# Attention steps kept behind the drains of first products, in a fused attention and feed-forward kernel

## The chip, the cores and the metric

The kernel runs on one core of one Trainium2 chip. The metric is the device time of one execution in microseconds, lower is better. The median of three runs before the change is 853.23 us (850.61 to 854.34).

## The reference

Linear attention over 8 batches, 8 heads, 576 positions and 64 columns a head, then a gated feed-forward layer over all 4608 tokens:

```python
q_s = exp(q - max(q, -1));          q_s /= sum(q_s, -1) + 1e-9
k_s = exp(k - max(k, 2));           k_s /= sum(k_s, 2) + 1e-9      # over the 576 positions
kv  = einsum('bhsd,bhse->bhde', k_s, v)
x   = einsum('bhsd,bhde->bhse', q_s, kv)      # -> (4608, 512)
h   = x @ w_in                                # 512 x 2048
g   = h * erf(softplus(h))
out = g @ w_out                               # 2048 x 512
```

Inputs and output are 32-bit floats.

## The kernel before

**Steps.** The tokens are cut into 12 blocks of 384 (two batches make three blocks), the 2048 middle columns into 4 groups of 512. That makes 48 steps, numbered n = 0 to 47, block by block. Steps 0 to 3 run in 32-bit floats while the weights are read in; from step 4 on each operand is split into a high and a low 16-bit half and a product is the sum of three. The feed-forward layer works a step at a time:

- `mm1(n, k)`, k = 0 to 3, is the first product, done in seven smaller ones (a Strassen form), each of twelve matmuls of 128x192. They go through three banks of PSUM, called Y, X and Z, in the order Y, X, Z, X, X, Z, X. A bank must be read out ("drained") into the tile H before its next product may start. VectorE drains Y (L1011), the first X (L1013), the third X (L1021) and the second Z (L1024); ScalarE copies out the first Z (L1016) and the second and fourth X (L1018, L1026).
- `softplus` and `erf` run on ScalarE (all from L344, each with a load of its table), `gmul` (L1079), `ghi` (L1093) and `glo` (L1097) on VectorE; the last two leave the two 16-bit halves of G in the space of H. These are the letters T, G, U, I and O.
- `mm2(n, tt)` is the second product, for three tiles of 128 tokens, twelve matmuls of 128x512 each (L1125).

While step n's first product runs, step n-2's second product does, one tile of it behind each quarter of the first.

**Attention.** One generator, `attention_rest`, gives the work of batches 1 to 7 in pieces. A token "A" draws one piece: the maxima of k (L497 to L501), their transposes on TensorE (L508, L521) and the reduction (km, L512), the maximum and subtraction of q (L454, L455), the subtraction from k (L662, L667), the exponentials on ScalarE, the products of k and v (L542) and their scale (kvbd, L595, L596), the sums of q (L461 to L467), the two halves of q (L640, L641) that SP transposes by a DMA (L643), and the products with q that give x (L632), which ScalarE copies into the x block (L443). q of the tail positions of two batches is called qt and is worked on with the odd batch. `load_kv` and `load_q`, the loads of the next batch, are issued within the same pieces, on SP's queue. `finish` then splits an x block into halves and the sums of the Strassen form (L297 on ScalarE, L298 and L388 on VectorE).

**What sets the order.** The program is written in the order of a hand-made string of tokens up to step 3, and then by the loop at the end, which draws attention pieces by `pace` behind each tile of `mm2`. That order is only a priority: a scheduler at build time puts the instructions of each engine into a fixed queue, letting one that is ready by its own reckoning pass one that stands ahead of it but is not. So a piece of attention may run long before the place where it is drawn. Each engine then runs its queue in order.

From about 112 us the weights are split too: `wsplit` and `wsplit_sums` (tokens S and R) put 16-bit halves of w_in (wi) and w_out (wo) in place, ScalarE the high half (L297), VectorE the low half (L298) and the sums (L322).


Of the kernel before, what the change touches and what calls it, by code (L numbers as in the profile page):

```python
# [1 line left out]

# [11 lines left out]
ALU = mybir.AluOpType  # L14
# [43 lines left out]
def attn_moe_kernel(  # L58
# [9 lines left out]
    nc = tc.nc  # L68
# [123 lines left out]
    def wdecode(i, part=None):  # L192


        jn, a = divmod(i, NPC)
        if jn not in stg:
            if wjobs[jn] in raw_place:
                stg[jn] = raw_place[wjobs[jn]][:, :4096].bitcast(F32)
            else:
                stg[jn] = xp.tile([P, 2048], F32, tag="x7", name=f"sg_{jn}")  # L200
        d = stg[jn][:, a * 1024:(a + 1) * 1024].bitcast(I32)
        if part is None:
            r = raws[i].rearrange("p a n -> p (a n)").rearrange("p (n two) -> p n two", two=2)
        else:
            r = raws[i][:, :, 512 * part:512 * part + 512].rearrange(
                "p a (n two) -> p a n two", two=2
            )
            d = d.rearrange("p (a n) -> p a n", a=2)[:, :, 256 * part:256 * part + 256]
        lo, hi = r[..., 0], r[..., 1]
        nc.vector.tensor_scalar(  # L210
            d, hi, 5, 2, op0=ALU.logical_shift_left, op1=ALU.logical_shift_right,
        )
        nc.vector.scalar_tensor_tensor(
            d, lo, 29, d, op0=ALU.logical_shift_right, op1=ALU.bitwise_or
        )
        nc.vector.scalar_tensor_tensor(
            d, hi, -(2**30), d, op0=ALU.bitwise_and, op1=ALU.bitwise_or
        )
        if part == 0:
            return  # L220
        raws.pop(i)
        slots.append(held.pop(i))
        slots.sort(key=lambda x: x[1])
        wload()
# [5 lines left out]
    def wop(jn, h, i, n):  # L230

        o = h * WIN + i * 512
        return wplace[wjobs[jn]][:, o:o + n * 512].rearrange("p (n c f) -> p n c f", n=n, c=2)
# [5 lines left out]
    def wsquares(jn):  # L239

        which, g = wjobs[jn]
        o = NG * (which == "out") + g
        for i in range(4):
            nc.scalar.activation(
                sqs, stg[jn][:, i * 512:(i + 1) * 512], AF.Square, accum_out=sq4[:, o, i:i + 1]
            )
        wsq.add(jn)
# [52 lines left out]
    def wsplit(jn):  # L300


        which, g = wjobs[jn]
        s = w_s[which][:, g:g + 1]
        assert "all" in wready and not raws

        assert all(wplace[wjobs[jn]] is not raw_place.get(wjobs[j]) for j in stg)
        if which == "out":
            split2(stg.pop(jn), whalf(jn, 0), whalf(jn, 1), s)
            wdone(jn)  # L310
            return
        sg = stg[jn].rearrange("p (c f) -> p c f", c=4)
        A = {(i, j): sg[:, 2 * j:2 * j + 2, 256 * i:256 * i + 256]
             for i in range(2) for j in range(2)}
        hi, lo = (wop(jn, h, 0, 2).rearrange("p n c f -> p (n c) f") for h in range(2))
        split2(sg[:, :, :256], hi, lo, s)
        split2(A[1, 1], wop(jn, 0, 2, 1)[:, 0], wop(jn, 1, 2, 1)[:, 0], s)
        for o, x, y, op in (
            ((1, 1), (1, 0), (1, 1), ALU.add), ((1, 0), (0, 0), (1, 0), ALU.subtract),
            ((0, 0), (1, 1), (0, 0), ALU.subtract), ((0, 1), (0, 1), (0, 0), ALU.subtract),  # L320
        ):
            nc.vector.tensor_tensor(A[o], A[x], A[y], op=op)  # L322

    def wsplit_sums(jn):
        which, g = wjobs[jn]
        sg = stg.pop(jn).rearrange("p (c f) -> p c f", c=4)
        for i in range(2):
            hi, lo = (
                wop(jn, h, 3 + 2 * i, 2).rearrange("p n c f -> p (n c) f") for h in range(2)
            )  # L330
            split2(sg[:, :, 256 * i:256 * i + 256], hi, lo, w_s[which][:, g:g + 1])
        wdone(jn)
# [14 lines left out]
        return i  # L347

    emitted = set()


    bat = [dict() for _ in range(B)]
# [461 lines left out]
    def attention_rest():  # L814
        for b in range(1, B):
            yield from attention(b) if b < E32 else attention16(b)

    att = attention_rest()

    def warm(n):  # L820

        z = ident.bitcast(F16)
        wm = pso.tile([P, 512], F32, tag="o2", name=f"warm_{n}")
        for _ in range(2 * n):
            nc.tensor.matmul(wm[:, :256], z[:, :P], z, start=True, stop=True)
# [149 lines left out]
    def mm1(n, k):  # L975

        p, bk, g = seq[n]
        s = st[n]  # L980
        assert ("in", g) in wready
        x = x7[p * NBK + bk]
        jn = wjobs.index(("in", g))
        Th = T // 2
        if k == 0:
            s["H"] = ch.tile([P, FG, T], F32, tag="H", bufs=3, name=f"H_{n}")
        C = {(i, j): s["H"][:, 2 * i:2 * i + 2, Th * j:Th * j + Th]
             for i in range(2) for j in range(2)}

        def prod(b, wi, xi):  # L990
            new = b not in s
            if new:
                s[b] = psh.tile([P, 512], F32, tag=f"p{b}", name=f"p{b}_{n}")
            w = [wop(jn, h, wi, 1)[:, 0] for h in range(2)]
            for a in range(2):
                o = s[b][:, a * Th:(a + 1) * Th]
                for c in range(2):
                    for i, (wl, xl) in enumerate(((0, 0), (0, 1), (1, 0))):
                        nc.tensor.matmul(  # L999
                            o, w[wl][:, c, a * P:(a + 1) * P], x[:, xl, xi, c, :],  # L1000
                            start=(new and a == 0 and c == 0 and i == 0),
                            stop=(c == 1 and i == 2), skip_group_check=True,
                        )

        def bank2(b):
            return s[b][:, :T].rearrange("p (a t) -> p a t", a=2)

        add = nc.vector.tensor_tensor
        if k == 0:
            prod("Y", 1, 1)  # L1010
            nc.vector.tensor_copy(C[0, 0], bank2("Y"))  # L1011
            prod("X", 0, 0)
            add(C[0, 0], bank2("X"), C[0, 0], op=ALU.add)  # L1013
        elif k == 1:
            prod("Z", 6, 3)
            nc.scalar.copy(C[1, 1], bank2("Z"))  # L1016
            prod("X", 3, 6)
            nc.scalar.copy(C[0, 1], bank2("X"))  # L1018
        elif k == 2:
            prod("X", 5, 5)  # L1020
            add(C[1, 1], bank2("X"), C[1, 1], op=ALU.add)  # L1021
        else:
            prod("Z", 4, 2)
            add(C[0, 1], bank2("Z"), C[0, 1], op=ALU.add)  # L1024
            prod("X", 2, 4)
            nc.scalar.copy(C[1, 0], bank2("X"))  # L1026

# [124 lines left out]
    def tok(name):  # L1152

        if name != "A":
            if name in done:
                return
            done.add(name)
        if name in steps:
            dep, f = steps[name]
            assert all(x in emitted_steps for x in dep.split()), name  # L1160
            f()
            emitted_steps.add(name)
            if all(f"y{c}" in emitted_steps for c in range(NC4)):
                bat[0]["xdone"] = True
            return
        c = name[0]
        if c == "A":
            r = next(att, None)
            share[0] += r or 0
            return r  # L1170
        x = [int(i) for i in name[1:].split(".")] if name[1:] else []
        if c == "w":
            warm(*x)
        elif c == "D":
            wdecode(NPC * x[0] + x[1], *x[2:])
        elif c == "Q":
            wsquares(*x)
        elif c == "S":
            wsplit(*x)
        elif c == "R":  # L1180
            wsplit_sums(*x)
        elif c == "f":
            xready(x_next[0])
            finish(x[0] % 2)
        elif c == "Z":
            wscales()
        elif c == "m":
            (mm1_32 if x[0] < NG else mm1)(*x)
            emitted.add(("m", *x))
        elif c == "M":  # L1190
            mm2(*x)
            emitted.add(("M", *x))
        else:
            fn[c](*x)

    def xready(i):

        p, bk = divmod(i, NBK)
        for b in [(2 * p,), (2 * p, 2 * p + 1), (2 * p + 1,)][bk]:
            while "xdone" not in bat[b]:  # L1200
                assert tok("A"), i
# [18 lines left out]
    for o in ORDER.split():  # L1220
        tok(o)
# [54 lines left out]
```

## Time and profile before

| | |
|---|---|
| median of three runs | 853.23 us |
| the profiled execution | 853.86 us |
| its span, first to last instruction | 851.7 us |
| mean granted TensorE clock | 0.988 |
| TensorE busy | 811.2 us (95%) |
| VectorE busy | 638.2 us (75%) |
| ScalarE busy | 503.0 us (59%) |
| GpSimd busy | 17.6 us (2%) |
| moved by DMA | 62.59 MB |

The busy times are shares of the whole span; a line of the profile such as "DVE H L1021 <- PE pX L999" says that VectorE's instruction of line 1021, writing H, waited for TensorE's of line 999, writing pX. PE is TensorE, PEld its weight loads, DVE VectorE, ACT ScalarE, POOL GpSimd, SPq the DMA queue of SyncE.

### The profile page before, as it was taken

To read this page: it belongs to the slowest core of one execution; us is meant where nothing else is said; L and a number is where in the kernel's file an instruction comes from. 1 tells how busy PE (TensorE), PEld (TensorE's weight loads), DVE (VectorE), ACT (ScalarE), POOL (GpSimd) and SP (SyncE) were. 2 spreads that over 40 slices of the span, in tenths; PEclk is the share of its full clock that TensorE was granted. 3 is DMA by queue.
4 is the path that set the end of the run, shared out by engine and by line. 5 is a ranking of instruction groups with operands and counts; after the bars stand their busy time and mean duration, and the time that the engine had idled before them with its cause. 6 is when DMAs were issued, how large, how long until landed. Compare 5 with 4: busy or idle time off the path is not lost.

```text
span 851.7 us, 15370 instructions
## 1 busy us (share of the span) xinstructions
PE 811.2 (95%) x6448; PEld 553.8 (65%) x6448; DVE 638.2 (75%) x913; ACT 503.0 (59%) x633; POOL 17.6 (2%) x37
## 2 busy tenths in 40 slices
PE   2999998899999999999999999999999999999997
PEld 1655557567667667766776676766776676777673
DVE  5999899998997879758865779748866657554543
ACT  2598486777564556555673566555663565543532
POOL 2010000000000000000000000000000000000000
PEclk8899999899999999999999999999999999999999
DMA  9997420016416402412134302322121000100100
GB/s 255 407 250 197 120 75 13 1 25 112 106 35 131 108 9 61 103 31 51 51 70 98 87 14 51 93 51 51 38 51 38 38 2 1 38 1 1 38 1 37
DMA packets 145508, 62.59 MB, mean 73 GB/s; under 512 B 134688, under 2 KB 136736, under 8 KB 145440
## 3 DMA queue, kind: packets, MB, share of 16 engines
q1 hardware_dynamic: 143264, 53.23, 25.1%
q0 software_dynamic: 2176, 8.39, 2.8%
q8 instruction: 50, 0.82, 0.4%
q14 instruction: 18, 0.15, 0.1%
HBM read 45.09 MB, written 9.44 MB: 64 GB/s over the span
## 4 chain that ended last, share of the span: by engine, by line
PE 64%; DVE 19%; ACT 10%; issue 3%; SPq 2%; DMA 1%; ACTq 0%; POOL 0%; DVEq 0%
PE o L1125 27%; PE pX L999 15%; PE pZ L999 7%; ACT G L344 4%; PE o L1116 4%; ACT L344 3%; PE pY L999 3%; DVE G L1079 3%; PE kv L542 2%; DVE H L1097 2%; PE pX L1038 2%; DVE H L1093 2%; SPq L409 2%; PE x L632 1%; DVE wi L298 1%
## 5 line engine op out<-in xcount | busy, mean ns | idle before, releaser
L1125 PE MATMUL o<-wo,H 128*128 128x512 f16 x1584 | 367.0, 380 | 2.8 <-DVE H L1093 1.8
L999 PEld LDWEIGHTS <-wi 128*128 128x128 f16 x3696 | 311.2, 98 | 44.3 <-issue 15.7
L1125 PEld LDWEIGHTS <-H 128*128 128x128 f16 x1584 | 152.7, 98 | 157.4 <-DVE H L1093 2.6
L999 PE MATMUL pX<-x,wi 128*128 128x192 f16 x2112 | 206.2, 248 | 7.6 <-ACT H L1018 4.5
L344 ACT ACT_TABLE_LOAD x104 | 133.4, 1283 | 2.8 <-DVE H L1024 0.8
L1079 DVE SCALAR_TENSOR_TENSOR G<-G,small,H 128x1536 f32<-128x1536 f32 x44 | 79.9, 1817 | 56.2 <-ACT G L344 56.0
L1026 ACT COPY H<-pX 128x384 f32<-128x384 f32 x44 | 20.9, 475 | 165.3 <-PE pX L999 159.9
L999 PE MATMUL pZ<-x,wi 128*128 128x192 f16 x1056 | 104.0, 247 | 3.4 <-ACT x L297 1.8
L344 ACT ACTIVATE G<-H,U 128x768 f32<-128x768 f32 (+1 forms) x60 | 72.7, 1231 | 22.1 <-DVE H L1024 21.5
L1097 DVE TENSOR_TENSOR H<-G,H 128x1536 f16<-128x1536 f32 x44 | 77.2, 1755 | 1.0
L344 ACT ACTIVATE G<-G 128x1536 f32<-128x1536 f32 x48 | 71.2, 1484 | 0.5
L999 PE MATMUL pY<-x,wi 128*128 128x192 f16 x528 | 51.9, 247 | 0.0
L1024 DVE TENSOR_TENSOR H<-pZ,H 128x384 f32<-128x384 f32 x44 | 24.4, 554 | 32.5 <-PE pZ L999 32.1
L1011 DVE COPY H<-pY 128x384 f32<-128x384 f32 x44 | 24.3, 553 | 30.3 <-PE pY L999 30.3
L1116 PE MATMUL o<-wo,G 128*128 128x512 f32 x96 | 43.4, 597 | 0.0
L1093 DVE CAST H<-G 128x1536 f16<-128x1536 f32 x44 | 42.1, 957 | 0.8
L297 ACT ACTIVATE x<-x 128x768 f16<-128x768 f32 (+1 forms) x44 | 32.9, 763 | 12.8 <-DVE x L388 11.1
L1141 DVE TENSOR_SCALAR ob<-o,V 128x512 f32<-128x512 f32 x29 | 21.7, 748 | 24.5 <-PE o L1125 24.5
L298 DVE SCALAR_TENSOR_TENSOR x<-x,x 128x768 f16<-128x768 f32 (+1 forms) x44 | 37.0, 851 | 3.2 <-ACT x L297 3.2
L1013 DVE TENSOR_TENSOR H<-pX,H 128x384 f32<-128x384 f32 x44 | 24.4, 554 | 15.9 <-PE pX L999 15.7
L443 ACT ACTIVATE x<-x 128x384 f32<-128x384 f32 (+1 forms) x52 | 17.5, 394 | 30.0 <-PE x L632 27.4
L1116 PEld LDWEIGHTS o<-wo,G 128*128 128x128 f32 x96 | 17.5, 190 | 18.7 <-issue 18.2
(184 smaller groups left out, 762.7 us busy)
## 6 DMA issues: line engine op xcount, KB each, us to landing
out_dram<-ob SPq DMA_DIRECT2D x32, 256.0 KB, 2.4
vbuf<-in_v_dram SPq DMA_DIRECT2D x60, 128.0 KB, 3.1
q<-in_q_dram SPq DMA_DIRECT2D x56, 128.0 KB, 3.4
k<-in_k_dram SPq DMA_DIRECT2D x56, 128.0 KB, 3.1
wo<-in_moe_w_in_dram SPq DMA_DIRECT2D x4, 1024.0 KB, 17.2
wi<-in_moe_w_out_dram POOLq DMA_DIRECT2D x2, 1024.0 KB, 8.9
wi<-in_moe_w_in_dram SPq DMA_DIRECT2D x2, 1024.0 KB, 9.4
raw<-in_moe_w_out_dram POOLq DMA_DIRECT2D x2, 1024.0 KB, 8.0
```

The source lines that it names most:

```text
L297: nc.scalar.activation(hi, src, AF.Copy, scale=s)
L298: nc.vector.scalar_tensor_tensor(lo, src, s, hi, op0=ALU.mult, op1=ALU.subtract)
L344: i = nc.scalar.activation(out_, in_, func, **kw)
L999: nc.tensor.matmul(o, w[wl][:, c, a * P:(a + 1) * P], x[:, xl, xi, c, :], start=(new and a == 0 and c == 0 and i == 0), stop=(c == 1 and i ...
L1011: nc.vector.tensor_copy(C[0, 0], bank2("Y"))
L1013: add(C[0, 0], bank2("X"), C[0, 0], op=ALU.add)
L1024: add(C[0, 1], bank2("Z"), C[0, 1], op=ALU.add)
L1079: nc.vector.scalar_tensor_tensor(flat(s["G"]), flat(s["G"]), (GB if n in OUT32 else GA)[:, g:g + 1], flat(s["H"]), op0=ALU.mult, op1=ALU.mult,
L1093: nc.vector.tensor_copy(flat(s["gh"]), flat(s["G"]))
L1097: nc.vector.tensor_tensor(flat(s["gl"]), flat(s["G"]), flat(s["gh"]), op=ALU.subtract)
L1116: nc.tensor.matmul(o, s["G"][:, a, ts_], w[:, a, :], start=(first_ and a == 0), stop=(last_ and a == FG - 1),)
L1125: nc.tensor.matmul(o, s[gt][:, a, ts_], w[wl][:, a, :], start=(first_ and a == 0 and i == 0), stop=(last_ and a == FG - 1 and i == 2),)
```

## The change

Three drains that VectorE does are remembered as they are written: Y of k = 0, the third X of k = 2, and the second Z of k = 3. Whenever a piece of attention is drawn, every VectorE instruction in it gets an edge to the last one remembered, without a semaphore: the scheduler may not put it in VectorE's queue ahead of that drain. Pieces drawn before step 4's first product, those of batch 1, have nothing remembered and stay as they were; so do the token lists for splits and `finish`, and the attention's instructions on other engines.

```diff
+    drained = [None]
...
         if k == 0:
             prod("Y", 1, 1)
-            nc.vector.tensor_copy(C[0, 0], bank2("Y"))
+            drained[0] = nc.vector.tensor_copy(C[0, 0], bank2("Y")).ins
...
         elif k == 2:
             prod("X", 5, 5)
-            add(C[1, 1], bank2("X"), C[1, 1], op=ALU.add)
+            drained[0] = add(C[1, 1], bank2("X"), C[1, 1], op=ALU.add).ins
         else:
             prod("Z", 4, 2)
-            add(C[0, 1], bank2("Z"), C[0, 1], op=ALU.add)
+            drained[0] = add(C[0, 1], bank2("Z"), C[0, 1], op=ALU.add).ins
...
         if c == "A":
-            r = next(att, None)
+            with tc.issue_after(drained[0]) if drained[0] is not None else nullcontext():
+                r = next(att, None)
```

No instruction is added on any engine but for rows that the listing groups otherwise. What moves is the order, and with it that of the other engines, since the scheduler reckons all of them together. Lines from 350 on are one higher in the changed kernel, from 1169 on two. In the names below H_895, H_1011, H_1129, H_1304 are the tiles H of steps 4, 5, 6 and 7, H_2432 and H_2697 those of steps 13 and 14, G_n the tile G that goes with the H behind the arrow.

The first place is ScalarE's queue at the start of step 4. x_1 is x block 1, wo_95 the place of a group of output weights. Before:

```order
L297 ACTIVATE x_1_837<-x_138 128x768
L297 ACTIVATE wi_90<-wi_91,small 128x512
L297 ACTIVATE x_1_837<-x_138 128x768
L1016 COPY H_895<-pZ_924 128x2x192
L297 ACTIVATE wi_90<-wi_91,small 128x1024
L1018 COPY H_895<-pX_910 128x2x192
L297 ACTIVATE wi_90<-wi_91,small 128x1024
L297 ACTIVATE wi_91<-wi_92,small 128x1024
L297 ACTIVATE wi_91<-wi_92,small 128x512
L1016 COPY H_1011<-pZ_1041 128x2x192
L1026 COPY H_895<-pX_910 128x2x192
```

And in the changed kernel, on the same engine from the same place:

```order
L297 ACTIVATE wi_90<-wi_91,small 128x512
L297 ACTIVATE wo_95<-wo_96,small 128x2048
L297 ACTIVATE x_1_837<-x_138 128x768 x2
L297 ACTIVATE wi_90<-wi_91,small 128x1024
L1017 COPY H_895<-pZ_924 128x2x192
L297 ACTIVATE wi_90<-wi_91,small 128x1024
L1019 COPY H_895<-pX_910 128x2x192
L297 ACTIVATE wi_91<-wi_92,small 128x1024
L297 ACTIVATE wi_91<-wi_92,small 128x512
L1027 COPY H_895<-pX_910 128x2x192
```

The split of an output weight has moved from some thirty rows later to a place ahead of both splits of x block 1, and the copy of step 5's first Z (H_1011) has left; it now stands eight rows further down, behind step 4's softplus and erf.

The second place is VectorE's queue between the halves of step 5 and those of step 6. x_2 and x_791 belong to x block 2, km, q_0 and k_0 to batch 2. Before:

```order
L1024 TENSOR_TENSOR H_1129<-pZ_1184,H_1129 128x2x192
L298 SCALAR_TENSOR_TENSOR x_2_1159<-x_791,x_2_1159 128x768
L298 SCALAR_TENSOR_TENSOR x_2_1159<-x_791,x_2_1159 128x384
L1097 TENSOR_TENSOR H_1011<-G_1122,H_1011 128x1536
L388 TENSOR_TENSOR x_791<-x_791 128x2x192
L1011 COPY H_1304<-pY_1305 128x2x192
L388 TENSOR_TENSOR x_791<-x_791 128x2x192
L1013 TENSOR_TENSOR H_1304<-pX_1319,H_1304 128x2x192
L388 TENSOR_TENSOR x_791<-x_791 128x2x192
L662 TENSOR_TENSOR k_0_592<-k_0_592,kB_1346 128x1024
L388 TENSOR_TENSOR x_791<-x_791 128x2x192
L1079 SCALAR_TENSOR_TENSOR G_1297<-G_1297,small,H_1129 128x1536
```

And in the changed kernel:

```order
L1098 TENSOR_TENSOR H_1011<-G_1122,H_1011 128x1536
L389 TENSOR_TENSOR x_791<-x_791 128x2x192
L513 TENSOR_REDUCE km_1264<-kT_1259 128x4
L389 TENSOR_TENSOR x_791<-x_791 128x2x192
L455 TENSOR_REDUCE q_0_m<-q_0_800 128x16
L389 TENSOR_TENSOR x_791<-x_791 128x2x192
L456 TENSOR_TENSOR q_0_800<-q_0_800,q_0_m 128x1024
L389 TENSOR_TENSOR x_791<-x_791 128x2x192
L298 SCALAR_TENSOR_TENSOR x_2_1159<-x_791,x_2_1159 128x768
L1025 TENSOR_TENSOR H_1129<-pZ_1184,H_1129 128x2x192
```

Step 6's last sum, which stood three rows ahead of step 5's low half, now stands nine rows behind it, and the reduction of km and the maximum and subtraction of q, done much earlier before, stand between.

The third place is VectorE's queue in step 14. x_4 is x block 4, q_0 and q_1 the halves of batch 4's q. Before:

```order
L454 TENSOR_REDUCE q_0_m<-q_0_2638 128x16
L298 SCALAR_TENSOR_TENSOR x_4_2727<-x_1809,x_4_2727 128x768
L455 TENSOR_TENSOR q_0_2638<-q_0_2638,q_0_m 128x1024
L1079 SCALAR_TENSOR_TENSOR G_2693<-G_2693,small,H_2432 128x1536
L298 SCALAR_TENSOR_TENSOR x_4_2727<-x_1809,x_4_2727 128x768
L1093 CAST H_2432<-G_2693 128x1536
L454 TENSOR_REDUCE q_1_m<-q_1_2655 128x16
L1097 TENSOR_TENSOR H_2432<-G_2693,H_2432 128x1536
L1021 TENSOR_TENSOR H_2697<-pX_2712,H_2697 128x2x192
```

And in the changed kernel:

```order
L298 SCALAR_TENSOR_TENSOR x_4_2727<-x_1809,x_4_2727 128x768
L1080 SCALAR_TENSOR_TENSOR G_2693<-G_2693,small,H_2432 128x1536
L298 SCALAR_TENSOR_TENSOR x_4_2727<-x_1809,x_4_2727 128x768
L1094 CAST H_2432<-G_2693 128x1536
L1098 TENSOR_TENSOR H_2432<-G_2693,H_2432 128x1536
L1022 TENSOR_TENSOR H_2697<-pX_2712,H_2697 128x2x192
```

The three pieces of attention ahead of the third X drain have gone behind it, to the next step. From step 16 on TensorE's own queue is the same in both but for a few rows; on VectorE attention goes on to stand a few rows later.

More of the change, by code (lines that the diff above doesn't have):

```diff
@@ L1 @@
-from contextlib import ExitStack
+from contextlib import ExitStack, nullcontext
 import concourse.bass as bass
```

## The prediction

> **What bounds the kernel now.** I read the cores first, then busy time by stretch, then what TensorE waits for, then the order of time around its longest waits.
>
> ```profile
> core 0: 851.7 us, clock 0.988
> ...
> core 0: us, PE busy (x) PEld busy (x) DVE busy (x) ACT busy (x) POOL busy (x), PEclk, DMA share, GB/s
> ...
> 120.00:162.00 42.00, 33.56 (x234) 24.45 (x234) 40.41 (x52) 31.60 (x40) 0.96 (x1) 0.88 0.11 32
> 162.00:822.00 660.00, 651.12 (x5621) 459.16 (x5620) 481.38 (x677) 386.53 (x453) 3.16 (x10) 1.00 0.22 51
> ```
>
> The second of the rows, from 162 us, holds most of the span: TensorE is busy 651.1 of 660 us at full clock, VectorE 481. The first, 120 to 162 us, is the other way round: VectorE 40.4 of 42, TensorE 33.6, its clock 0.88. There the weights are split and the first half-precision steps start, and VectorE is the bound. The last two attention-free steps show the floor of a step:
>
> ```profile
> 733.49 2.59 PE o L1125 x12
> ...
> 748.18 2.59 PE o L1125 x12
> ...
> PE pX L999 <- ACT H L1018: 4.5, 2, 4.2
> ...
> DVE k L497 <- DMA k<-in_k_dram: 5.2, 3, 2.3
> ...
> PE pX L999 <- DVE H L1021: 1.5, 3, 0.9
> PE pX L999 <- ACT H L1026: 1.3, 2, 0.6
> ```
>
> The same group of twelve second products comes 14.69 us apart: nothing to be had there but by less work. The waits are small. The drains of first products, which the change puts in front of attention, cost TensorE 4.5 + 1.5 + 1.3 = 7.3 us in the whole run, 4.2 of them in one wait. So a change of order can gain a few us at most, unless it also shortens 120 to 162 us; and it can lose there, where VectorE has no idle time.
>
> **The change, part by part.** No instruction's work is added or taken away; no DMA is added. Every price is a place in VectorE's queue, so I follow three places, by the orders quoted above.
>
> *Head, the weight split in front.* VectorE's first batch 2 work is gone from before step 4:
>
> ```profile
> 126.42 0.69 DVE L497 TENSOR_TENSOR k<-k 128x512 f32<-128x512 f32 x1
> 127.02 1.21 DVE L454 TENSOR_REDUCE q_m<-q 128x16 f32<-128x1024 f32 x1
> ...
> 125.42 2.02 ACT L297 ACTIVATE wo<-wo,small 128x2048 f16<-128x2048 f32 x1
> ...
> 134.09 1.07 PE L999 MATMUL pZ<-x,wi 128*128 128x192 f16 x11 [1.28 <-DVE x L298]
> ...
> 135.20 0.48 ACT L1016 COPY H<-pZ 128x384 f32<-128x384 f32 x1 [2.68 <-PE pZ L999]
> ...
> 191.81 2.25 DVE L298 SCALAR_TENSOR_TENSOR wo<-wo,small,wo 128x2048 f16<-128x2048 f32 x1
> ...
> 152.79 2.08 PE L999 MATMUL pX<-x,wi 128*128 128x192 f16 x12 [4.19 <-ACT H L1018]
> ```
>
> What takes the room is splits of output weights: on ScalarE one of 2.02 us now stands ahead of the last two splits of x block 1, whose second half TensorE waits for at 134.09. Late by 2.0, caught up in the 2.68 us that ScalarE idles behind it. VectorE's half of that split (2.25, now run at 191.81) comes in ahead of step 4's third X drain, where one k maximum of 0.69 leaves: 2.25 - 0.69 = 1.6 at most, 1.3 if a few of the tenths that VectorE waits there are filled. Step 4's last product starts that much later. Then ScalarE's copy of step 5's first Z bank stands behind the erf of step 4, and TensorE, which now asks for that bank ahead of the products of 152.79, waits as it does now for the copy behind it: its 4.2 us wait stays, shifted by about 1 us. I book +1.3 by 178 us, and nothing for the pieces of attention that left: they come back below.
>
> *Head, x block 2 and step 6.*
>
> ```profile
> 171.79 0.55 DVE L1024 TENSOR_TENSOR H<-pZ,H 128x384 f32<-128x384 f32 x1
> ...
> 173.59 1.75 DVE L1097 TENSOR_TENSOR H<-G,H 128x1536 f16<-128x1536 f32 x1
> 175.26 0.55 DVE L388 TENSOR_TENSOR x<-x 128x384 f32<-128x384 f32 x1
> 175.73 0.55 DVE L1011 COPY H<-pY 128x384 f32<-128x384 f32 x1
> ...
> 161.45 0.68 DVE L512 TENSOR_REDUCE km<-kT 128x4 f32<-128x512 f32 x1
> ...
> 173.97 1.76 ACT L344 ACTIVATE G<-H,U 128x768 f32<-128x768 f32 x2
> 175.75 1.28 ACT L344 ACT_TABLE_LOAD   x1
> 177.05 1.49 ACT L344 ACTIVATE G<-G 128x1536 f32<-128x1536 f32 x1
> ...
> 179.19 1.81 DVE L1079 SCALAR_TENSOR_TENSOR G<-G,small,H 128x1536 f32<-128x1536 f32 x1
> ...
> 182.66 0.95 DVE L1093 CAST H<-G 128x1536 f16<-128x1536 f32 x1
> ...
> 186.39 1.74 DVE L1097 TENSOR_TENSOR H<-G,H 128x1536 f16<-128x1536 f32 x1
> ...
> 189.57 1.67 PE L1125 MATMUL o<-wo,H 128*128 128x512 f16 x7
> ...
> 194.32 0.69 PE L542 MATMUL kv<-vbuf,k 128*64 128x65 f32 x16
> ...
> 195.63 1.17 PE L999 MATMUL pZ<-x,wi 128*128 128x192 f16 x12
> ```
>
> Today the last sum of step 6 (L1024, 171.79) runs before step 5's low half (L1097, ends 175.3). In the new order it comes after that, after four differences of x (0.47 each, the distance of 175.26 and 175.73), the reduction for km (0.68), batch 2's q maximum and its subtraction (1.21 each by the row at 127.02) and a split of x (0.87). That is 1.88 + 0.68 + 2.42 + 0.87 = 5.9 us, less some 0.3 of overlap at the starts: it ends at 175.3 + 5.6 + 0.5 = 181.4, with L1097 where it is now. ScalarE's second half of the softplus waits for it: 0.9, then table 1.28 and erf 1.49 bring 185.1. VectorE then has L1079 1.81, kt 0.68, L1093 0.95, three attention pieces of 1.2 and L1097 1.74: 193.9, with 0.6 of small ones 194.5, where it now ends at 188.1. TensorE now reads that low half with its third product, at 190.0 (189.57 + 2 x 0.216, the twelfth part of 2.59). It would be held 4.5 us; but the new order moves the second kv product (194.32 to 195.63, 1.3 us) in front, so 3.2 remain. This wait swallows the +1.3 before it, since it hangs on VectorE and not on where TensorE was. Lower end 0, if VectorE reaches 181 some 3 us earlier by idle time I don't see; upper end 9.6 us (181.4 less 171.8) less the 1.9 slack and 1.3: +6.4. I take **+3.2**.
>
> *Later, the drains.*
>
> ```profile
> 255.17 1.07 PE L999 MATMUL pX<-x,wi 128*128 128x192 f16 x11 [0.34 <-ACT H L1018]
> ...
> 305.40 1.21 DVE L454 TENSOR_REDUCE q_m<-q 128x16 f32<-128x1024 f32 x1
> 306.52 1.75 DVE L1097 TENSOR_TENSOR H<-G,H 128x1536 f16<-128x1536 f32 x1
> 308.19 0.55 DVE L1021 TENSOR_TENSOR H<-pX,H 128x384 f32<-128x384 f32 x1
> ...
> 308.80 1.15 PE L999 MATMUL pX<-x,wi 128*128 128x192 f16 x12 [0.86 <-DVE H L1021]
> ...
> 343.53 1.15 PE L999 MATMUL pX<-x,wi 128*128 128x192 f16 x12 [0.64 <-ACT H L1026]
> ...
> 288.09 0.23 PE L632 MATMUL xt<-qt,kvbd 128*128 128x64 f16 x2 [0.94 <-DVE kvbd L595]
> ```
>
> At step 14 the q maximum (1.21) leaves the queue ahead of L1021, and that sum is then over before the bank is asked for: the wait of 0.86 goes, -0.9. Step 11's copy on ScalarE (0.34) comes 0.5 earlier, as a cast stands behind it now: -0.3. At 343.53, and one period later, ScalarE's copy waits behind a split of x, which waits for VectorE; a cast of k and q now stands ahead of that difference, so I book -0.2 each of the 0.64, not the whole. At 288.09 a maximum of k (0.69) enters the chain from the scale to kvbd, and five first products of about 0.08 come in ahead of the wait: +0.3, or 0.4 with the other wait of that place. Nothing is booked for the loads that SP issues behind the pinned steps. They go out later, as do the maxima that read them, and VectorE waits for such loads of k today, 5.2 us in three places, with TensorE busy: a maximum that comes later waits less. A load as late as the step itself shifts nothing. What is late next is the transposes of qt, a rival below. Sum -1.2, bounds -3.0 (the three drains' waits and the one at 288.09 gone, the second period's too) and +1.5 (0.69 in each of two more chains).
>
> **The sum**: +3.2 - 1.2 = +2.0. The profiled execution took 853.86 us, 2.2 beyond its span; it would take 855.9. The median of the runs shown is 853.23, 0.6 below it, so 855.2 beside that.
>
> [...] The row of 152.79 shows 2.08 us for twelve products that take 1.15 elsewhere, right behind 4.19 us of idle; the mean clock of that stretch is 0.88. [...]
>
> **Rivals.**
>
> ```profile
> 156.15 2.12 PE L999 MATMUL pX<-x,wi 128*128 128x192 f16 x12
> ```
>
> - *Faster: the head runs smoother.* If the order breaks the 4.19 us wait up and step 6 is in time, TensorE gains 3.4 of it and 1.9 of the two slow groups (2.08 and 2.12 for 1.15 each), with the drains' -1.2: 853.2 - 6.5 = 846.7. For it: batch 2's maxima (0.69 and 1.21 among them) have left VectorE ahead of step 5. Against: as much weight splitting has come in its place. It decides at 152.8: the wait must fall under about 1 us.
> - *No loss in the head.* VectorE reaches step 6 early enough for the 1.9 us of slack and the moved kv product: 853.2 - 1.2 = 852.0.
> - *Slower by more: the upper end.* Step 6's delay shows in full and steps 7 and 8 inherit some: +6.4 - 1.2, 858.4, with another 1.5 from one drain per late step 860. It decides at L1024 of step 6: if it ends after 184 us.
> - *Late transposes in the odd batches.* The last piece of qt is now pinned behind a drain, and its transpose on SP's queue behind that, so that TensorE could stand still for it in batches 3, 5 and 7.
>
> ```profile
> qt<-kt SPq DMA_TRANSPOSE x3, 3.1
> ```
>
> It takes 3.1 us to land; where it is issued only as TensorE gets there, it costs that less the 0.94 waited at 288.09 anyway, 2.2, and three times 6.5: 861. At half, 858. Against: in batches 5 and 7 the order leaves two groups of second products (2.59 each) and four of first ones between.
>
> **How the numbers follow.** Forecast, 853 to 857.4: 0.46. No loss: 0.25. Faster: 0.07. Slower cases together: 0.22. About 0.5%, 4.3 us, is what can be told from no change here; so faster is below 849.0, slower above 857.5. Same takes the first two, 0.71. The range leaves out the lower part of the faster case and the upper part of the slower ones, some 0.15: 849.5 to 859.5. The likeliest case gives 855.2.
>
> **What would show it.** In the changed kernel's trace: L1024 of step 6 (the third of its line) near 181 instead of 171.8; the third L1097 ending near 194; TensorE idle in front of the third group of second products; step 14's wait for L1021 gone; two waits for L1026 of about 0.4; TensorE's busy time after 200 us unchanged but for that. I am wrong if the third L1097 ends before 190, if the wait near 153 is under 3 us, or if TensorE waits for a transpose after 400 us.

## The result, and the profile after

The changed kernel takes 859.96 us (median of 6 runs, 858.73 to 861.49), the kernel before 853.57 us beside it: a ratio of 1.0085, 95% interval 1.0069 to 1.0101. It is slower, by 7.3 us by the ratio (the two medians lie 6.4 us apart); 855.2 was forecast, and the range ended at 859.5. The profiled execution took 861.49 us, with a span of 859.4.

The core, then the same two stretches as before (us; busy time of TensorE, its weight loads, VectorE, ScalarE, GpSimd; TensorE's clock; DMA share; GB/s):

```profile
core 0: 859.4 us, clock 0.992
...
120.00:162.00 42.00, 31.70 (x214) 23.74 (x213) 40.46 (x49) 30.47 (x38) 0.96 (x1) 0.84 0.11 32
162.00:822.00 660.00, 646.99 (x5574) 455.41 (x5572) 483.74 (x679) 381.15 (x449) 3.17 (x10) 1.00 0.22 51
```

VectorE is as full as it was up to 162 us (40.46 of 42, before 40.41), TensorE does 1.9 us less there, and then 4.1 us less than before in the next 660. What it waits for (line waited for: us in all, times, longest):

```profile
PE pZ L1000 <- ACT H L1017: 4.7, 1, 4.7
...
PE pZ L1000 <- ACT x L297: 3.7, 1, 3.7
PE pX L1000 <- ACT H L1019: 3.6, 4, 1.5
PE xt L633 <- DMA qt<-kt: 1.6, 2, 1.1
...
PE pX L1000 <- ACT H L1027: 1.1, 2, 0.5
PE pX L1000 <- DVE H L1022: 1.0, 2, 0.7
```

The wait of 4.2 at 152.8 has become one of 4.7 for the first Z's copy, and one of 1.78 us for a split of x block 1 (at 132.57 before) one of 3.7. Before, that row was:

```profile
132.57 0.24 PE L999 MATMUL pZ<-x,wi 128*128 128x192 f16 x1 [1.78 <-ACT x L297]
```

New are waits of up to 1.5 us for L1019, the copy of the fourth product, at 423 and 618 us, which stood nowhere in the forecast. To see where the time went, I take the start of each step's first product (the first pY row of the step), subtract that of the kernel before, and see by how much the difference grows over a stretch of steps; a gain is negative:

| stretch | after, minus before, us | forecast |
|---|---|---|
| steps 4 to 10 | +4.27 | +3.2 (the head) |
| steps 10 to 18 | -0.53 | -0.9 (step 14), -0.3 (step 11), -0.2, +0.4 (batch 3) |
| steps 18 to 23 | +1.72 | 0 |
| steps 23 to 32 | -0.03 | -0.2 |
| steps 32 to 35 | +1.73 | 0 |
| steps 35 to 47 | -0.01 | 0 |

(The rest of 7.41 us at step 47, 0.27, lies before step 4.) So the head came out 1.1 us above its forecast, and two losses of 1.7 us each, at steps 20 to 21 and 32 to 33, are what was not seen. The rows of the first of them, in the changed kernel (start, duration, engine, line):

```profile
409.49 0.55 DVE L1022 TENSOR_TENSOR H<-pX,H 128x384 f32<-128x384 f32 x1
...
409.96 1.21 DVE L455 TENSOR_REDUCE q_m<-q 128x16 f32<-128x1024 f32 x1
...
411.09 0.68 DVE L513 TENSOR_REDUCE km<-kT 128x4 f32<-128x512 f32 x1
...
411.69 1.21 DVE L456 TENSOR_TENSOR q<-q,q_m 128x1024 f32<-128x1024 f32 x1
...
412.82 0.55 DVE L1025 TENSOR_TENSOR H<-pZ,H 128x384 f32<-128x384 f32 x1
...
413.44 1.28 ACT L344 ACT_TABLE_LOAD   x1 [1.68 <-DVE H L1025]
...
420.79 2.00 ACT L344 ACTIVATE k<-k 128x1024 f32<-128x1024 f32 x2
422.70 0.46 ACT L1019 COPY H<-pX 128x384 f32<-128x384 f32 x1
...
423.20 1.15 PE L1000 MATMUL pX<-x,wi 128*128 128x192 f16 x12 [1.52 <-ACT H L1019]
...
618.47 1.15 PE L1000 MATMUL pX<-x,wi 128*128 128x192 f16 x12 [1.52 <-ACT H L1019]
```

Batch 5's first q is pinned behind step 20's third X sum (L1022), so its maximum and subtraction stand between that and the step's last sum (L1025). ScalarE waits 1.68 us for that sum, its softplus and erf are late, step 21's copies stand behind the erf (that of the fourth product also behind a second exponential of k, some 0.9 us, which follows it in the kernel before), and TensorE waits 1.52 us for the bank of the fourth product. Twelve steps later the same (618.47). The same place in the kernel before:

```profile
406.41 0.69 DVE L512 TENSOR_REDUCE km<-kT 128x4 f32<-128x512 f32 x1
...
407.01 0.55 DVE L1024 TENSOR_TENSOR H<-pZ,H 128x384 f32<-128x384 f32 x1
...
407.64 1.28 ACT L344 ACT_TABLE_LOAD   x1
...
415.95 0.46 ACT L1018 COPY H<-pX 128x384 f32<-128x384 f32 x1
...
416.46 1.15 PE L999 MATMUL pX<-x,wi 128*128 128x192 f16 x12
```

Only km's reduction stands there, ScalarE starts without a wait, and TensorE gets its bank in time. The forecast's own two places, in the changed kernel: the head (wo is VectorE's low half of an output weight's split, the row at 195.58 the third group of second products going on with the low half of G) and step 14.

```profile
127.75 2.35 DVE L298 SCALAR_TENSOR_TENSOR wo<-wo,small,wo 128x2048 f16<-128x2048 f32 x1 [0.75 <-ACT wo L297]
...
134.76 0.24 PE L1000 MATMUL pZ<-x,wi 128*128 128x192 f16 x1 [3.70 <-ACT x L297]
...
178.08 1.21 DVE L455 TENSOR_REDUCE q_m<-q 128x16 f32<-128x1024 f32 x1
...
179.67 1.22 DVE L456 TENSOR_TENSOR q<-q,q_m 128x1024 f32<-128x1024 f32 x1
...
182.14 0.55 DVE L1025 TENSOR_TENSOR H<-pZ,H 128x384 f32<-128x384 f32 x1
...
193.69 1.75 DVE L1098 TENSOR_TENSOR H<-G,H 128x1536 f16<-128x1536 f32 x1
...
195.58 2.55 PE L1126 MATMUL o<-wo,H 128*128 128x512 f16 x11
...
311.77 0.55 DVE L1022 TENSOR_TENSOR H<-pX,H 128x384 f32<-128x384 f32 x1
...
312.82 1.15 PE L1000 MATMUL pX<-x,wi 128*128 128x192 f16 x12
```

Step 6's last sum is at 182.14 (forecast 181.4, before 171.79), its low half over at 195.4 (forecast 194.5), and at 312.82 the wait of 0.86 for the third X sum is gone.

### The profile page after: what moved, and what is told of

It reads as the page before. It is cut to its first block, busy times and chain, and to the rows that moved or that the text cites. A ratio compares the mean times of both kernels' runs of the same rounds, so it can differ in the third digit from the quotient of the medians.

```text
span 859.4 us, 15376 instructions
## 1 busy us (share of the span) xinstructions
PE 813.1 (95%) x6448; PEld 555.5 (65%) x6448; DVE 640.9 (75%) x913; ACT 503.1 (59%) x633; POOL 17.6 (2%) x37
## 4 chain that ended last, share of the span: by engine, by line
PE 60%; DVE 18%; ACT 15%; issue 3%; SPq 2%; DMA 1%; ACTq 0%; POOL 0%; DVEq 0%
PE o L1126 25%; PE pX L1000 14%; PE pZ L1000 7%; ACT G L344 6%; ACT L344 5%; PE o L1117 3%; DVE G L1080 3%; PE pY L1000 3%; PE kv L543 2%; DVE H L1098 2%; PE pX L1039 2%; PE x L633 2%; DVE H L1094 1%; DVE x L298 1%; SPq L410 1%
## 5 line engine op out<-in xcount | busy, mean ns | idle before, releaser
L1025 DVE TENSOR_TENSOR H<-pZ,H 128x384 f32<-128x384 f32 x44 | 24.3, 553 | 33.7 <-PE pZ L1000 33.6
```

The lines of the kernel that those rows point to most:

```text
L1025: drained[0] = add(C[0, 1], bank2("Z"), C[0, 1], op=ALU.add).ins
```

## The experiments

All are edits of the changed kernel on the line numbers of the kernel before (L1018 is the fourth product's copy, L1024 the last sum, L1021 the third X sum). `at_n` is the step whose first product was written last. The ratios are to the kernel before, with their 95% intervals; the changed kernel's is 1.0085. The last column is worked out as in the table above, each from its one profiled execution.

| | ratio | interval | steps 4-10, 10-18, 18-23, 32-35, us |
|---|---|---|---|
| changed | 1.0085 | 1.0069 to 1.0101 | +4.27, -0.53, +1.72, +1.73 |
| e1 batch 2 free | 1.0033 | 1.0016 to 1.0050 | +0.01, -0.49, +1.72, +1.72 |
| e2 batch 2 alone | 1.0058 | 1.0035 to 1.0081 | +4.26, +1.64, +0.11, +0.02 |
| e3 q free in 5, 7 | 1.0041 | 1.0026 to 1.0057 | +4.11, -0.53, +0.03, +0.05 |
| e4 copy first | 1.0079 | 1.0057 to 1.0100 | +4.23, -0.52, +1.64, +1.65 |
| e5 q free in 2 | 1.0054 | 1.0034 to 1.0074 | +1.80, -0.49, +1.72, +1.72 |
| e6 pin Y only | 1.0011 | 0.9999 to 1.0023 | +2.89, -1.06, -0.17, -0.16 |
| e7 step 15 only | 0.9984 | 0.9970 to 0.9999 | -0.51, -1.51, +0.09, +0.04 |
| e8 late, q free | 1.0003 | 0.9990 to 1.0017 | +0.02, -0.50, +0.03, +0.04 |
| e9 wo split late | 1.0126 | 1.0110 to 1.0142 | +5.81, -0.55, +1.73, +1.73 |
| e10 Y from 15 | 0.9987 | 0.9973 to 1.0001 | +1.00, -1.38, -0.17, -0.16 |
| e11 wo_94 behind x1 | 1.0075 | 1.0052 to 1.0099 | +4.40, -0.52, +1.72, +1.71 |

e7 and e10 run the order of the kernel before in steps 4 to 10 (e1 and e8 up to 203 us), so the column's first number differs by -0.5 to +1.0 us between executions of one order. TensorE's granted clock goes with it: over the first 48 us of step 4 it is 0.93 in e7, 0.89 in the kernel before, e1 and e8, and 0.86 in e10. The other numbers repeat within a few hundredths.

**Theory:** the loss is two things. In the head, batch 2's attention, pinned behind step 6's drains, makes step 6's last sum late. In steps 20 and 32 the first q of batches 5 and 7 does the same. **Rivals:** the late waits are the head's loss seen again; or any pin crowds VectorE, wherever it is.

*e1 and e2, the two halves.*

```diff
-            with tc.issue_after(drained[0]) if drained[0] is not None else nullcontext():
+            pin = drained[0] is not None and at_n[0] >= 9     # e2: at_n[0] < 9
+            with tc.issue_after(drained[0]) if pin else nullcontext():
```

> Nothing is pinned while step 8 or an earlier one is under way, so batch 2 goes as in the kernel before; batches 3 to 7 are pinned. Theory (two separate losses: 4.2 us in the head by step 6's late last sum, 3.4 us by two waits of TensorE for ScalarE's copy of the fourth product, X of steps 21 and 33): the head's loss goes, the two waits stay at about 1.5 each, and the time is 1.7 to 2.7 us over the kernel before. Rival (the head's loss is only handed on, and later waits are the same idle time seen again): the later waits shrink with it, and the time is within 1 us of the kernel before.

> The other half: pinned only while step 8 or an earlier one is under way, so batch 2 alone is pinned. Theory: step 6's last sum stays at about 182 us and its low half ends at about 195; the time is 3.5 to 4.7 us over the kernel before, with no wait for the fourth product's copy at 420 or 615 us. Rival (the loss of the head is made up by idle time later on): under 2 us over.

e1 is 2.8 us over (0.33% of 852), e2 4.9 us over, together 7.7, about what the change costs (7.3). In e1 the head's +4.27 is gone and the two later losses stand unchanged at 1.72; in e2 the head stays and they are gone. They are two separate things: the first rival falls. (e2 has +1.64 in steps 10 to 18, as it doesn't get step 14's gain and waits 1.31 us there for L1021.)

*e3, the piece with the first q of batches 5 and 7 not pinned.*

```diff
+        free[0] = b in (5, 7)
         yield next(sh)
         km = k_max_T(b, kmax)
         q_sub(rows(qs[0]), 16, f"q_{b}_0")
+        free[0] = False
...
+            pin = drained[0] is not None and not free[0]
```

> As changed, but the one piece of batches 5 and 7 that holds km and the first q's maximum and subtraction is not pinned. By the order VectorE then runs those two (2.4 us) a step earlier, ahead of the last sum of step 19 and 31, and nothing of q stands between the third X sum and the last sum of steps 20 and 32. Theory (these two rows alone make the last sum 1.7 us late, softplus and erf with it, and TensorE waits for the copy queued behind the erf): both waits of 1.5 us go, and the time is 3.0 us over the kernel before, 3.4 under the changed kernel. Rival (VectorE is too full everywhere once attention stands late; another drain is late instead): at most 1 us under the changed kernel.

3.5 us over the kernel before, 0.44% (3.7 us) under the changed one. The timeline of e3 at step 20:

```profile
407.80 0.55 DVE L1024 TENSOR_TENSOR H<-pZ,H 128x384 f32<-128x384 f32 x1
...
409.02 1.28 ACT L344 ACT_TABLE_LOAD   x1
...
417.33 0.46 ACT L1018 COPY H<-pX 128x384 f32<-128x384 f32 x1
...
417.90 1.15 PE L999 MATMUL pX<-x,wi 128*128 128x192 f16 x12
```

No wait of ScalarE, none of TensorE. The order differs from the changed kernel's by these rows and what follows from them at the two places alone, so two rows of VectorE (1.21 each) in the wrong one of two slots are the whole 3.4 us. What follows from them is also that ScalarE's copy comes ahead of the second exponential and four of TensorE's second products behind the bank's first products; e4 has these two moves without VectorE's, and keeps the loss. The second rival falls.

*e4, ScalarE's copy ahead of the second exponential.* The exponentials of batches 5 and 7 behind k's first half are collected and issued in `mm1(n, 1)` right behind the copy of L1018.

```diff
             nc.scalar.copy(C[0, 1], bank2("X"))
+            [f() for f in late]; late.clear()
...
-            act(t, t, AF.Exp, chain=b > 1)
+            f = lambda t=t: act(t, t, AF.Exp, chain=b > 1)
+            late.append(f) if b in (5, 7) and t is not ks[0] else f()
```

> As changed, but in batches 5 and 7 the exponentials of the second half of k and of what follows it are issued behind ScalarE's copy of the fourth product of steps 21 and 33 instead of ahead of it; VectorE's and TensorE's queues stay. Theory: of the 1.7 us that TensorE loses at each place, the exponential ahead of the copy makes 0.94 and the late last sum the rest, so that the wait falls from 1.5 to about 0.6 and the time by 1.9 us under the changed kernel. Rival 1 (the late sum alone): the wait stays at 1.5, no change. Rival 2 (the order on ScalarE alone): the wait goes, 3.4 us under the changed kernel.

No gain to speak of: 0.08 us at each place. Against the changed kernel this tells little. e4's profiled execution runs 2.47 us ahead of the changed kernel's at step 18, so its copy (419.28 against 422.70) is 0.95 earlier; and yet TensorE waits 1.45 us:

```profile
415.60 2.75 PE L1125 MATMUL o<-wo,H 128*128 128x512 f16 x12
...
419.28 0.46 ACT L1018 COPY H<-pX 128x384 f32<-128x384 f32 x1
...
419.80 1.15 PE L999 MATMUL pX<-x,wi 128*128 128x192 f16 x12 [1.45 <-ACT H L1018]
```

TensorE's queue did not stay, as I had written: four second products (0.86 us), which the changed kernel has ahead of this wait, came behind it. TensorE started to wait as much earlier as the copy came. Against e3 it tells more: by their traces, from 80 us on, ScalarE's and TensorE's queues stand in the same order in e3 and e4, and VectorE's differs at the two places alone. There e3 loses 0.03 and 0.05 us, e4 1.64 and 1.65. So VectorE's rows by themselves make 1.6 of the 1.7 at each place. What the order on ScalarE would do with TensorE's queue held still stays open.

*e5, the q pieces of batch 2 not pinned* (as e3, with b = 2, and `q_sub` of the second q too).

> As changed, but the two pieces of batch 2 with the maxima and subtractions of q (and km) are not pinned. The early part of the head stays as in the changed kernel by the order (the split of an output weight ahead of x block 1's on ScalarE, TensorE held 3.7 us there); of the rows between the third X sum and the last sum of step 6 the first q's maximum and subtraction go, two of four differences of x and one split of x too: 2.4 + 0.9 + 0.9 = 4.2 us. Theory (the head's loss hangs on step 6's last sum, and the early delay is swallowed): the last sum at about 178 us instead of 182, the low half over at about 191.5 instead of 195.4, and the time 3 us under the changed kernel, some 4 over the kernel before. Rival (the early delay of 2.9 us carries through by itself): the last sum comes earlier, and the time is at most 1.5 us under the changed kernel.

2.6 us under the changed kernel by the ratios, 2.5 by the head's column (+1.80). Its last sum and low half of step 6:

```profile
174.90 0.55 DVE L1024 TENSOR_TENSOR H<-pZ,H 128x384 f32<-128x384 f32 x1
...
187.21 1.75 DVE L1097 TENSOR_TENSOR H<-G,H 128x1536 f16<-128x1536 f32 x1
```

With 1.9 us added, by which this execution starts step 4 ahead of the changed kernel's, 176.8 and 190.9: the last sum 5.3 us earlier, more than the rows that left. The loss shrinks with it; a rest of 1.8 us remains. Where TensorE loses its time in the head is looked at behind e11.

*e6, only the first drain remembered.*

```diff
-            drained[0] = add(C[1, 1], bank2("X"), C[1, 1], op=ALU.add).ins
+            add(C[1, 1], bank2("X"), C[1, 1], op=ALU.add)
...
-            drained[0] = add(C[0, 1], bank2("Z"), C[0, 1], op=ALU.add).ins
+            add(C[0, 1], bank2("Z"), C[0, 1], op=ALU.add)
```

> As changed, but only the first drain (Y, of k = 0) is remembered; a piece drawn later in the step is pinned behind that one too. By the order step 6's last sum still comes behind km and the q subtraction (only the q maximum has left), step 14's third X sum still has no attention ahead of it, and in steps 20 and 32 the q maximum and subtraction run ahead of the third X sum and no longer between it and the last. Theory: the loss of steps 20 and 32 is due to the pin behind the third X sum alone: both waits go, 3.4 us under the changed kernel, and up to 1.2 more at step 6; 2.6 to 3.8 over the kernel before. Rival (any pin crowds VectorE there, whichever drain it is): another wait of 1 us or more stands in steps 19 to 21 and 31 to 33, at most 1.5 under the changed kernel.

Better than the theory had it: 0.9 us over, and its interval includes no difference. Steps 18 to 23 and 32 to 35 turn from +1.72 to -0.17, the waits for L1026 at steps 16 and 28 fall from 0.54 to 0.14, and the head loses 2.89 instead of 4.27. It is the pin behind the third X sum that costs. The one behind the last sum does nothing: by the loop that draws the pieces, none is drawn between that sum and the next step's first drain.

*e7 and e10, what of the change is worth keeping.* e7 pins only the pieces drawn while step 15 is under way (`at_n[0] == 15`), e10 is e6 from step 15 on (`at_n[0] >= 15`).

> The kernel before, with only the pieces pinned that are drawn while step 15 is under way: batch 4's maxima and subtractions of k and q. By the order they leave VectorE's queue ahead of step 14's third X sum and nothing else changes but a few rows of steps 15 to 17. Theory: step 14's wait of 0.86 us goes and no new one comes: 0.9 us under the kernel before (852.7 to 852.3 where that takes 853.5). Rival (the pieces come back in front of a later drain, as in steps 6 and 20): no gain, or up to 1 us over it.

> The kernel before up to step 14; from step 15 on attention is pinned behind the first drain (Y) alone. Theory, from the traces of the runs before: step 14's wait of 0.86 us goes, the two waits of 0.64 for the sixth copy (X of steps 16 and 28) shrink or go, no wait comes at steps 20 and 32; 2.0 us under the kernel before (851.2 where that takes 853.2), 0.6 under the kernel with step 15 alone. Rival (what step 15 alone gives is all): 0.9 to 1.4 us under the kernel before.

e7 is 0.16% (1.4 us) under the kernel before, the interval just clear of 1; e10 is 0.13% under, and its interval reaches 1. In e7 TensorE's bank is ready at step 14:

```profile
304.03 0.55 DVE L1021 TENSOR_TENSOR H<-pX,H 128x384 f32<-128x384 f32 x1
...
305.34 1.15 PE L999 MATMUL pX<-x,wi 128*128 128x192 f16 x12
```

By the steps e7 gains 1.51 there, more than the 0.9: one wait of 0.64 for L1026 goes as well. e10 gains 1.38, 0.17, 0.43 (steps 23 to 32) and 0.16, 2.1 in all, as expected by the trace; the times don't tell it from e7. Both beat the changed kernel. e7 beats the kernel before by little, and that e10 does is not shown by its times.

*e8, both repairs together.*

> The two repairs together: nothing pinned before step 9, and the q piece of batches 5 and 7 free. Theory (losses add up: 4.2 in the head, 3.4 in steps 20 and 32, and a gain of 0.9 at step 14 against some 0.7 of new waits for x's scale and q's tail in batch 3): 0.2 us under the kernel before, within what can be told of no difference. Rival (a further loss spread over the pinned steps): 1.5 us or more over it.

1.0003: no difference, as the sum of the parts had it (-0.44 us from step 4 on). No further loss is spread over the pinned steps.

*e9 and e11, the early delay.* TensorE waits 3.70 us for x block 1 at 134.76 in the changed kernel. The prediction put that down to ScalarE's split of the last output weight ahead of it. e9 holds that split (and what follows from it) behind step 5's last copy; e11 instead holds VectorE's low half of the third output weight behind x block 1's last low half.

```diff
-            split2(stg.pop(jn), whalf(jn, 0), whalf(jn, 1), s)
+            # e9: step 5's L1026, job 7; e11: x block 1's last L298, job 6
+            with tc.issue_after(held) if jn == JOB else nullcontext():
+                split2(stg.pop(jn), whalf(jn, 0), whalf(jn, 1), s)
```

> As changed, but ScalarE's split of the last output weight (2.02 us) is held behind step 5's last copy, so it no longer stands ahead of x block 1's second half; VectorE's half of it follows, still ahead of step 6's last sum. Theory (of the head's two delays the larger shows, and that is step 6's last sum): TensorE's wait for x block 1 falls from 3.7 to about 1.8 us, step 6's last sum stays within 1.5 us of where it is, and the time is at most 1.3 us under the changed kernel, 5.5 to 7 over the kernel before. Rival (the two delays add up): 2 us or more under the changed kernel.

Theory and rival both fall: e9 is 0.4% over the changed kernel (1.5 us by the steps), and the wait is what it was. Only that the last sum stays within 1.5 us holds.

```profile
132.74 0.84 ACT L297 ACTIVATE x<-x 128x768 f16<-128x768 f32 x1 [1.75 <-DVE x L388]
...
134.77 0.24 PE L999 MATMUL pZ<-x,wi 128*128 128x192 f16 x1 [3.70 <-ACT x L297]
...
183.58 0.55 DVE L1024 TENSOR_TENSOR H<-pZ,H 128x384 f32<-128x384 f32 x1
```

With the split gone, ScalarE simply idles 1.75 us for x block 1's differences (L388): VectorE is late, not ScalarE. Up to step 6's last sum VectorE does as much work as in the changed kernel (50.8 and 50.7 us from the start of step 4) but idles 3.8 us instead of 2.5, and that sum is 1.4 later. So the row to suspect is VectorE's of 127.75, 2.35 us, ahead of those differences:

> As changed, but VectorE's low half of the third output weight's split (2.35 us at 127.75 in the changed kernel, ahead of x block 1's differences) is held behind x block 1's last low half. It then runs some 8 us later, and as much of VectorE's work as before stands ahead of step 6's last sum. Theory (TensorE's wait of 3.70 for x block 1 comes from that row; the head's loss is set by VectorE's work ahead of step 6's last sum, the early delay is swallowed): the wait falls to about 1.8, the last sum of step 6 stays at 181 to 183 us and the time within 1 us of the changed kernel, 6 to 7 us over the kernel before. Rival (the early delay adds to it): 2 us or more under the changed kernel.

```profile
132.25 0.24 PE L999 MATMUL pZ<-x,wi 128*128 128x192 f16 x1 [1.57 <-ACT x L297]
...
136.38 2.34 DVE L298 SCALAR_TENSOR_TENSOR wo<-wo,small,wo 128x2048 f16<-128x2048 f32 x1
...
146.19 1.15 PE L999 MATMUL pX<-x,wi 128*128 128x192 f16 x12 [1.83 <-DVE H L1013]
...
181.97 0.54 DVE L1024 TENSOR_TENSOR H<-pZ,H 128x384 f32<-128x384 f32 x1
```

The wait falls to 1.57, step 6's last sum stays (181.97), and the time stays too (1.0075 against 1.0085, the head +4.40). What TensorE no longer loses at that wait it loses later, at 146.19 among others, and still ahead of step 6's last sum.

*Where the head's loss lies.* TensorE's work from step 4's start to step 10's, in the first 48 us (to 177 us) and behind them. Before:

```profile
128.65:176.65 48.00, 39.00 (x329) 30.98 (x328) 46.29 (x60) 35.91 (x41) 0.00 (x0) 0.89 0.02 6
176.65:224.92 48.27, 47.10 (x423) 32.16 (x421) 44.58 (x72) 29.34 (x39) 0.63 (x2) 1.00 0.43 90
```

And in the changed kernel:

```profile
128.92:176.92 48.00, 37.33 (x319) 31.05 (x318) 45.48 (x57) 33.79 (x39) 0.00 (x0) 0.86 0.02 6
176.92:229.46 52.54, 49.83 (x433) 33.64 (x432) 46.56 (x74) 31.15 (x40) 0.64 (x2) 1.00 0.35 78
```

Of the 4.27 us, 1.67 are idle time in the first 48 us (10.67 against 9.00) and 1.54 idle time behind them (2.71 against 1.17). The other 1.05 are the same 752 products taking longer (87.16 against 86.11 us); as the clock is 1.00 behind the 48 us in both kernels and 0.86 against 0.89 in them, they lie in the first 48 us too. The same for the other runs, with the time of step 6's last sum and VectorE's work ahead of it, all counted from step 4's start:

| us | last sum of step 6 | VectorE busy until then | TensorE idle, first 48 us | idle behind | TensorE busy | loss to step 10 |
|---|---|---|---|---|---|---|
| before | 43.1 | 41.4 | 9.0 | 1.2 | 86.1 | 0 |
| e5 | 47.9 | 46.4 | 10.8 | 1.9 | 85.4 | 1.80 |
| e6 | 51.2 | 50.5 | 11.4 | 1.6 | 86.1 | 2.89 |
| changed | 53.2 | 50.7 | 10.7 | 2.7 | 87.2 | 4.27 |
| e11 | 53.4 | 51.3 | 10.1 | 2.5 | 88.2 | 4.40 |
| e9 | 54.7 | 50.8 | 11.0 | 3.5 | 87.6 | 5.81 |

The later the last sum, the larger the loss, and the sum comes when VectorE has done the work ahead of it, plus 0.7 to 3.8 us in which it idles. But more than half of the changed kernel's loss (2.7 of 4.27 us) has been made before that sum comes. That batch 2's pinned pieces cause the head's loss is shown by e1. That they do it through this one sum is argued from the table, in which each row is one execution and the clock differs by chance too (0.86, 0.89 and 0.93 in executions of one order, as above).

## Why the prediction was wrong, by its own steps

**The head, +3.2: measured +4.27 (4.1 to 4.3 in four executions whose head has this order).** The last sum of step 6 is late as forecast: 182.14 against 181.4, the low half over at 195.4 against 194.5, and the third group's product that first reads it (the fourth, not the third) at 195.58 against 194.5. But the forecast made of this one wait of TensorE, 3.2 us, which swallows the +1.3 before it. That did not come: 2.7 us had been lost by 177 us, ahead of that sum, and 1.5 us of idle time came behind it. So it is in part luck that the head's number came within 1.1 us. e11 does not show a swallowing either: its wait for x block 1 is 2.1 us shorter, but the time comes back as other waits and slower products ahead of the sum. Two details failed as well. The early delay came from VectorE's low half of an output weight, 2.35 us in front of x block 1's differences, and not from ScalarE's split; I had read ScalarE's queue, where the split stood ahead, without asking whether ScalarE would have been ready. The row that I quoted for it, 134.09, waits for VectorE's low half, and that wait stayed (1.28, now 1.22); the one that grew is the one of 1.78 at 132.57. And TensorE does not idle in front of the third group: it starts it at 190 and fills the time to 195.58 with first products and products of k and v; it idles before and behind that (3.70 at 134.76, 1.46 at 225.06).

**Step 14, -0.9: measured -0.9** (the difference falls from 4.93 to 4.03 between steps 14 and 15). The small terms: step 11's wait of 0.34 went, but a wait of 0.7 for the first X sum came near 254.8; the waits for L1026 at steps 16 and 28 shrank by 0.1 each, not 0.2; batch 3's products with qt wait 1.12 us for the transpose where they waited 0.94 for the scale, +0.2 instead of +0.4.

**The step that failed is "later, the drains", -1.2 with an upper bound of +1.5: measured +2.9.** I followed only the places where TensorE waits in the kernel before, and asked what the new order makes of them. Where it waits for nothing, I took VectorE's attention, a few rows later, as free, with no more reason than that TensorE's own queue stays nearly the same from step 16 on. The bound priced one k maximum (0.69) in each of two chains; the rows that came were two of 1.21 us, between a step's third X sum and its last, at two steps where only 0.7 us of other work had stood there. It was the very mechanism that I had worked out for step 6, and I did not look for it a second time. e3 and e4 together show that these rows make the two losses. With the head 1.1 us over its forecast and this step 4.1 us over, the sum of +2.0 became 7.1.

**The rivals.** Late transposes in odd batches: there, but in the place of the wait for the scale (1.12 us in batch 3; 0.46 in batch 7, at 675 us, where it waited 0.77), not on top of it. That was one of the three signs of being wrong, a wait for a transpose after 400 us; it came and cost nothing, and the other two did not come. No sign looked at the places that did cost. The upper end, 858.4 to 860, came out at its time for another reason: step 6's last sum is at 182.1, not behind 184, and little is inherited (counted from step 4, step 7's last sum is 5.9 us later than before and step 8's 4.5, where the shift itself is 4.3). The faster case's sign did not come: the wait at 152.8 was not broken up, as I had said against it, and TensorE's clock fell from 0.88 to 0.84 in that stretch. Its 1.9 us for the two slow groups are shown won back by no run: the twelve products near 153 us took 2.08 us behind the wait of 4.19 in the kernel before, of 4.65 in the changed one (with two others between) and of 3.73 in e11; 1.15 stand behind shorter waits at other places, of 0.64 (343.53 before) to 1.83 us (146.19 in e11).

## What to carry to other kernels

An edge that says "not before this drain" also says "in the slot behind it": what it holds back is put in front of the drain that comes next. So the new queue is to be walked at every place where held work lands between two drains, at the places that wait for nothing today above all, and its length there compared with the room that the next drain's reader has. Where one engine is full (VectorE to 162 us here, 40.4 of 42 us), a row comes when the work ahead of it in that queue is done, and a wait taken away elsewhere can come back in another place, as in e11. Pinning only where a wait was seen (e7) kept the gain and none of the loss, though the gain, 1.4 us, is hardly more than the runs can tell.

## What the runs showed of the hardware

Executions of the same order differ in when step 4 begins: 128.92 in the changed kernel's, 126.31 in e3's, 2.6 us apart, though up to there their queues are the same but for the place of one product of k and v. Most of it is there with the first products of k and v, 2.3 us apart:

```profile
18.24 1.14 PE L543 MATMUL kv<-vbuf,k 128*64 128x65 f32 x16 [4.00 <-ACT k L867]
```

```profile
15.98 0.84 PE L542 MATMUL kv<-vbuf,k 128*64 128x65 f32 x16 [2.65 <-ACT k L866]
```

So two executions are compared from a step on, not by their ends; what makes the difference is not shown here.

TensorE's products behind the wait of 3.70 us for x block 1 took 1.91 or 1.92 us for eleven, instead of 1.07, in all seven executions with a wait of 3.7 (3.70 to 3.77). Behind two waits of 1.78 and 1.28 us with one product between them they took 1.07 in three executions and 1.92 in two, in the same order; here e1's and e8's:

```profile
134.38 1.07 PE L999 MATMUL pZ<-x,wi 128*128 128x192 f16 x11 [1.28 <-DVE x L298]
```

```profile
133.76 1.92 PE L999 MATMUL pZ<-x,wi 128*128 128x192 f16 x11 [1.28 <-DVE x L298]
```

The granted clock shows three outcomes of the same two waits: it is 0.50 at once in e8 and e10, falls about 1 us later in e1 and the kernel before (there 1.00 up to 135.10, 0.50 from 135.20), and stays at 1.00 in e7 (mean of its whole execution 0.995, of the kernel before's 0.988). So behind these two waits, 3.06 us in all, the clock fell in four executions and stayed in one; what decides it is not shown here.
